# One run of scores and one run of outputs per chunk in place of four mixed runs, in decayed linear attention with a softplus feed-forward

## The chip, the cores and the metric

One core of a Trainium2 chip runs the whole kernel. The metric is the device time of one execution in microseconds (us); the time of a kernel is the median of its runs. Differences under about 0.2% are at the edge of what repeated runs can tell.

## The reference

Attention with a decay per head, computed block by block (block of 64 positions) with a state that is carried along the sequence, and then a feed-forward layer with softplus over all tokens. `q`, `k`, `v` are (4, 8, 768, 64): batch, heads, positions, head size.

```python
for b in range(nb):                       # nb = 768 / 64 blocks
    intra = einsum('bhic,bhjc->bhij', qb, kb) * Dmask        # scores in the block
    intra = einsum('bhij,bhjd->bhid', intra, vb)
    inter = einsum('bhid,bhde->bhie', qb * lam_pow, kv_state)
    out[block] = intra + inter
    kv_state = lam_block * kv_state + einsum('bhsd,bhse->bhde', kb * rev_pow, vb)
x = out as (4 * 768 tokens, 512)
h = x @ w_in                              # (512, 2048)
g = maximum(h, 0) + log1p(exp(-abs(h)))   # softplus
return g @ w_out                          # (2048, 512)
```

## The kernel before

**Tiling.** The sequence is cut into 6 chunks of 128 positions (two blocks of 64). In a chunk the 8 heads form 4 pairs. A *unit* `g` is one pair in one chunk, `g = 4 * chunk + pair`, 24 in all. Its `q`, `k`, `k` transposed and `v` for all 4 batches lie in one tile `att{g}`.

**The feed-forward part** goes in slots `s = 16 * chunk + f`, one for each chunk and each of 16 slices of the hidden layer. `mlp1(s)` (L344) makes `h` with 12 matmuls of 128x512; ScalarE takes the softplus into `l` (L334) and casts its high half into `g` (L338), VectorE subtracts to get the low half (L342); four slots later `mlp2(s)` (L358) adds 12 matmuls of 128x512 into the four banks `o` of the chunk, one for each batch. After the sixteenth slot of a chunk the four banks are copied out (L376) and stored. The split into a high and a low half is for precision: each product is made of three.

**The attention part** of a unit has these steps. `k_decay` (L262, ScalarE) scales the transposed keys. `mm_scores` (L276, L278, TensorE) makes the scores `x` and the sums for the state `y`, 64 small matmuls of 64x64. `mask_scores` (L297, VectorE) writes the masked scores over `k`. `update_states` (L302, VectorE) makes the state at the second block, and the state for the next chunk's unit of the same pair. `q_decay` (L267, VectorE) scales `q`. `mm_out` (L289, L293, TensorE) makes the outputs `z`, again 64 small matmuls. `x_high` and `x_low` (L318 on ScalarE, L325 on VectorE) split `z` into the input of the next chunk's `mlp1`.

**Buffers.** PSUM's 8 banks are divided for the whole program: four `o`, two `h`, and two as one tile `t` ("work"). In SBUF a pool of 22 tiles of 8 KB per partition holds units, weights, the inputs `x_{chunk}` and the output buffer `ob`; a pool of 7 tiles of 4 KB holds the `g`; one tile holds `l`; five hold states.

**What sets the order.** The program is written out in order; each engine does its own instructions in that order and waits by semaphores. The first stage (chunk 0, the conversion of the weights, the units of chunk 1) follows a table written out by hand (L476 to L505). From slot 17 on a loop (L517) works: every fourth slot it has an *event* for one unit `g`, in which TensorE does the outputs of unit `g - 1` and the scores of unit `g` one behind the other, and then an `mlp2` and two `mlp1`. So a chunk has four such mixed runs of small matmuls among its large ones, and attention is one chunk ahead of the feed-forward part. Transfers are issued from SP's queue in program order.

## Time and profile before

| | us |
|---|---|
| median of 3 runs | 595.84 |
| lowest and highest | 595.80 and 596.04 |
| the profiled execution | 595.62 |
| its span, first to last instruction | 593.8 |

The profiled execution has 1.8 us outside its span. The profile shows one execution. Engines are PE (TensorE's matmuls), PEld (its weight loads), DVE (VectorE), ACT (ScalarE), POOL (GpSimd) and SP (the queue that issues transfers). In its rows "L353" is line 353 of the kernel, `h<-x,w` names what is written and read, and "x12" counts instructions. In a timeline a row's start and its duration in us stand first; matmuls overlap in the array, so the distance between starts tells the pace, and not the duration of one (some 390 ns for a large one).

### The profile page before, as it was taken

How to read it: one execution, taken by the hardware profiler on the slowest of the kernel's cores; microseconds unless marked ns; L12 is line 12 of the kernel's file. 1: busy time of each engine (PE TensorE's matmuls, PEld its weight loads, DVE VectorE, ACT ScalarE, POOL GpSimd, SP SyncE). 2: the span in 40 equal slices, each digit the busy share in tenths (PEclk: the TensorE clock that was granted, in tenths of full speed). 3: DMA queues.
4: the chain of work that ended last, by engine and by line, in shares of the span. 5: the costliest groups of instructions: out<-in, count | busy, mean ns of one | idle time of the engine just before them, and what ended most of it. 6: DMA issues, size and time to landing. Idle time of an engine off the chain costs nothing.

```text
span 593.8 us, 11190 instructions
## 1 busy us (share of the span) xinstructions
PE 586.9 (99%) x5009; PEld 484.3 (82%) x5009; DVE 224.3 (38%) x338; ACT 210.0 (35%) x341; POOL 1.5 (0%) x9
## 2 busy tenths in 40 slices
PE   8999999999999999999999999999999999999997
PEld 6778888888888888888888888888888888888885
DVE  8999999623313134132232331312312211211011
ACT  5899867232233232322323213323232222222211
POOL 1000000000000000000000000000000000000000
PEclk9999999999999999999999999999999999999999
DMA  8999230214002106001022300220500000100001
GB/s 288 416 416 418 106 131 2 72 73 142 3 0 72 73 0 214 0 2 52 21 72 90 124 3 0 73 72 0 214 0 2 1 0 1 72 0 2 0 1 71
DMA packets 15759, 48.95 MB, mean 82 GB/s; under 512 B 1888, under 2 KB 1888, under 8 KB 15712
## 3 DMA queue, kind: packets, MB, share of 16 engines
q1 hardware_dynamic: 15344, 47.46, 21.4%
q10 hardware_dynamic: 368, 0.79, 0.4%
q8 instruction: 39, 0.64, 0.4%
q14 instruction: 8, 0.07, 0.0%
HBM read 41.95 MB, written 6.29 MB: 81 GB/s over the span
## 4 chain that ended last, share of the span: by engine, by line
PE 94%; DMA 3%; DVE 1%; SPq 1%; issue 0%; ACT 0%
PE o L370 45%; PE h L353 42%; PE x L276 2%; PE z L289 2%; PE z L293 2%; DMA att<-in_att 1%; DMA raw<-in_wts 1%; PE y L278 1%; DVE c L219 1%; DVE w L232 0%; DVE c L215 0%; DVE c L225 0%; PE y L440 0%; SPq L122 0%; PE w L276 0%
## 5 line engine op out<-in xcount | busy, mean ns | idle before, releaser
L370 PE MATMUL o<-w,g 128*128 128x512 f32 x1152 | 278.6, 392 | 0.0
L353 PE MATMUL h<-x,w 128*128 128x512 f32 x1152 | 274.5, 390 | 0.3 <-ACT x L417 0.3
L353 PEld LDWEIGHTS h<-x,w 128*128 128x128 f32 x1152 | 215.8, 188 | 46.4 <-DVE w L232 0.7
L370 PEld LDWEIGHTS o<-w,g 128*128 128x128 f32 x1152 | 214.8, 188 | 45.3
L342 DVE TENSOR_TENSOR g<-l,g 128x512 fp32r<-128x512 f32 x96 | 66.4, 692 | 305.3 <-ACT g L338 305.3
L334 ACT ACTIVATE l<-h 128x512 f32<-128x512 f32 x96 | 57.5, 598 | 310.9 <-PE h L353 308.6
L338 ACT CAST g<-l 128x512 fp32r<-128x512 f32 x96 | 59.6, 621 | 2.8
L302 DVE SCALAR_TENSOR_TENSOR st<-st,lam_c,y 64x256 f32<-64x256 f32 x68 | 29.9, 480 | 2.4 <-PE y L278 1.3
L297 DVE TENSOR_TENSOR att<-x,mask 128x512 f32<-128x512 f32 x19 | 13.1, 692 | 43.4 <-PE y L278 23.8
L318 ACT CAST x<-z 128x512 fp32r<-128x512 f32 x20 | 11.7, 585 | 41.4 <-PE z L293 41.4
L289 PEld LDWEIGHTS z<-att,st 64*64 64x64 f32 x640 | 17.0, 134 | 7.0 <-issue 6.3
L276 PE MATMUL x<-att 64*64 64x64 f32 x608 | 21.7, 219 | 0.0
L278 PE MATMUL y<-att 64*64 64x64 f32 x544 | 21.3, 219 | 0.0
L289 PE MATMUL z<-att,st 64*64 64x64 f32 x640 | 20.9, 224 | 0.0
L225 DVE CUSTOM_DVE_ANT_0 c<-raw,c 128x2048 uint16<-128x2048 uint16 (+1 forms) x19 | 20.0, 1054 | 0.3
L276 PEld LDWEIGHTS x<-att 64*64 64x64 f32 x608 | 20.1, 135 | 0.0
L232 DVE TENSOR_TENSOR w<-c,w 128x1024 fp32r<-128x1024 f32 (+1 forms) x19 | 20.0, 1055 | 0.1
L219 DVE SCALAR_TENSOR_TENSOR c<-raw,c 128x1024 uint32<-128x1024 uint32 (+1 forms) x19 | 20.0, 1053 | 0.0
L207 ACT ACTIVATE c<-raw 128x1024 f32<-128x1024 f32 (+1 forms) x19 | 18.9, 1006 | 3.1 <-DMA raw<-in_wts 3.1
L293 PE MATMUL z<-att 64*64 64x64 f32 x640 | 19.9, 218 | 0.0
L278 PEld LDWEIGHTS y<-att 64*64 64x64 f32 x544 | 19.6, 135 | 0.0
L211 ACT ACTIVATE raw<-raw 128x1024 uint32<-128x1024 uint32 (+1 forms) x19 | 19.1, 1013 | 1.2 <-DMA raw<-in_wts 1.2
(48 smaller groups left out, 172.6 us busy)
## 6 DMA issues: line engine op xcount, KB each, us to landing
att<-in_att SPq DMA_DIRECT2D x43, 512.0 KB, 4.9
raw<-in_wts SPq DMA_DIRECT2D x32, 512.0 KB, 9.2
out_dram<-ob SPq DMA_DIRECT2D x22, 256.0 KB, 2.3
att<-in_att SPq DMA_DIRECT2D x9, 256.0 KB, 7.5
out_dram<-ob ACTq DMA_DIRECT2D x2, 256.0 KB, 2.0
att<-in_att ACTq DMA_DIRECT2D x1, 256.0 KB, 4.7
lam_b<-in_lam SPq DMA_DIRECT2D x1, 4.0 KB, 2.8
```

Of the source, the lines that this page charges most:

```text
L219: nc.vector.scalar_tensor_tensor(out=c, in0=raw_at(ks, 1), scalar=0x80000000, in1=c, op0=ALU.bitwise_and, op1=ALU.bitwise_or)
L225: nc.vector.tensor_add(out=c, in0=c, in1=raw_at(ks, 0))
L276: nc.tensor.matmul(x[r, cols], lhsT=k[r, b, t], rhs=q[r, b, t], start=True, stop=True)
L278: nc.tensor.matmul(y[half(1 - s), cols], lhsT=kd[r, b, t], rhs=v[r, b, t], start=True, stop=True)
L289: nc.tensor.matmul(w[half(t), s, cols], lhsT=st[r, b, t], rhs=qd[r, b, t], start=True, stop=False)
L293: nc.tensor.matmul(w[half(t), s, cols], lhsT=v[r, b, t], rhs=a[r, b, t], start=False, stop=True)
L302: nc.vector.scalar_tensor_tensor(out=to[:, :, t], in0=of[:, :, t], scalar=lam_c[r, h : h + 1], in1=u[:, :, t], op0=ALU.mult, op1=ALU.add,)
L334: nc.scalar.activation(l_tiles[s], h_tiles.pop(s), AF.Softplus)
L338: nc.scalar.copy(out=g_tiles[s][:, 0, :], in_=l_tiles[s])
L342: nc.vector.tensor_sub(out=g[:, 1, :], in0=l_tiles.pop(s), in1=g[:, 0, :])
L353: nc.tensor.matmul(h_tiles[s], lhsT=w[:, i, cs], rhs=x[:, j, :], start=p == 0 and n == 0, stop=p == NP - 1 and n == 2,)
L370: nc.tensor.matmul(o_tiles[c][b], lhsT=g[:, i, b * 128 : (b + 1) * 128], rhs=w[:, j], start=f == 0 and n == 0, stop=f == NF - 1 and n == 2,)
```

## The change

In the loop the four events of a chunk become two.

- **Scores.** In the fourth slot of a chunk (`f == 3`), behind the last `mlp2` of the chunk before, TensorE does the scores and state sums of all four units of the next chunk (`chunk_scores`), 256 small matmuls. They fill all 8 banks: the two `h` for the first unit, the four `o` for the second and third, the work tile for the fourth. VectorE masks and updates unit by unit. The `mlp2` of the next slot is put off by one slot, since it needs the `o` banks.
- **States.** The two states of a unit are now written into the place of its transposed keys (`update_kept`): ScalarE copies the carried state there, VectorE makes the second one beside it.
- **Decays.** `k_decay` of the four units goes into slots 1 to 3 of the chunk, `q_decay` into slots 4 to 7.
- **Outputs.** In slot 8 TensorE does the outputs of all four units (`chunk_outs`), 256 small matmuls, two units to a pair of banks: the two `h`, and the work tile. Casts and subtractions then take a whole bank of two units at a time.
- **Loads.** Two units are loaded behind the outputs, the other two in slot 1 of the next chunk.
- **Output buffer.** It is made of four tiles of the 4 KB pool, in place of one of the 8 KB pool.
- **The table.** Its steps for unit 8 (`kd1 8`, `sc1 8`, `m1 8`, `up 8`, `qd 8`) are gone; the loop does them.

```diff
-    def mm_out(g, w):
+    def mm_out(g, w, first=0):
...
+    def update_kept(g, y):
+
+        u = y.rearrange("q (b t e) -> q b t e", b=B, t=2)
+        old, st = states[g], kt_of(g)
+        states[g] = st
+        nc.scalar.copy(out=st[lo], in_=old[lo])
+        decayed(g, st[hi], old[lo], lo, u[hi])
+        if not last_chunk(g):
+            states[g + NP] = th([128, B, 2, D], F32, f"st_{g + NP}")
+            decayed(g, states[g + NP][lo], st[hi], hi, u[lo])
+
+    def chunk_scores(c):
+
+        homes = [(bank, bank), (obank, obank), (obank, obank), None]
+        for g, home in zip(range(c * NP, c * NP + NP), homes):
+            if home:
+                xy[g] = [new(f"{name}{g}") for new, name in zip(home, "xy")]
+            else:
+                w = work(f"w{g}")
+                xy[g] = w[:, 0], w[:, 1]
+            mm_scores(g, *xy[g])
+
+    def chunk_outs(c):
+
+        homes = {0: [bank(f"z{c}_{s}") for s in range(2)]}
+        w = work(f"z{c}")
+        homes[1] = [w[:, s] for s in range(2)]
+        for p in range(NP):
+            mm_out(c * NP + p, homes[p // 2], p % 2 * 256)
...
+            for s in range(2):
+                nc.scalar.copy(out=x[:, 0, s], in_=of[s])
+            for s in range(2):
+                nc.vector.tensor_sub(out=x[:, 1, s], in0=of[s], in1=x[:, 0, s])
...
-            ob = t8([128, B, 512], F32, f"ob{c}")
+            ob = [t4([128, 2, 512], F32, f"ob{c}_{i}")[:, j] for i in range(2) for j in range(2)]
...
     for s in range(17, last + LAG):
-        if events.get(s + 1, NG) < NG:
-            run("kd1", events[s + 1])
+        c, f = divmod(s, NF)
+        first = (c + 1) * NP
+        if f == 1 and c < NCH - 1:
+            load_upto(first + NP)
+        if 1 <= f <= 3 and c < NCH - 1:
+            for g in ((first,), (first + 1,), (first + 2, first + 3))[f - 1]:
+                run("kd1", g)
...
-        if s in events:
-            g = events[s]
-            run("out1", g - 1)
-            if g < NG:
-                run("sc1", g)
...
+        if f != LAG or c == NCH:
+            mlp2_upto(s - LAG)
+        if f == LAG - 1 and c < NCH - 1:
+            chunk_scores(c + 1)
+            for g in range(first, first + NP):
+                mask_scores(g, xy[g][0])
+                update_kept(g, xy[g][1])
+        if f in range(LAG, 2 * LAG) and c < NCH - 1:
+            run("qd", first + f - LAG)
+        if f == 2 * LAG and c < NCH - 1:
+            chunk_outs(c + 1)
+            mlp2_upto(s - LAG + 1)
+            load_upto(first + NP + 2)
         if s < last:
             mlp1(s)
```

How this stands on the engines is shown at two places. First TensorE at the end of a run that has scores. Before, in the loop, the scores of unit 18 (`x18`, `y18`) end the mixed run, and one `mlp2` (into `o3`) and two `mlp1` (into `h56`, `h57`) follow:

```order
L276 MATMUL x18_3321<-att18_3175 64x64
L278 MATMUL y18_3322<-att18_3175 64x64
L370 MATMUL o3_0_3070<-w7_722,g53_3211 128x512 x3
L370 MATMUL o3_1_3071<-w7_722,g53_3211 128x512 x3
L370 MATMUL o3_2_3072<-w7_722,g53_3211 128x512 x3
L370 MATMUL o3_3_3073<-w7_722,g53_3211 128x512 x3
L353 MATMUL h56_3379<-x_3_0_2334,w6_573 128x512 x6
L353 MATMUL h56_3379<-x_3_1_2737,w6_573 128x512 x6
L353 MATMUL h57_3397<-x_3_0_2334,w7_722 128x512 x6
L353 MATMUL h57_3397<-x_3_1_2737,w7_722 128x512 x6
```

Now the scores of units 16 to 19 end with unit 19 in the work tile (`w19`); two `mlp1` (lines of the changed kernel: L391) take the two `h` banks, and then comes the `mlp2` that opens the chunk's `o3`:

```order
L276 MATMUL w19_3136<-att19_2934 64x64
L278 MATMUL w19_3136<-att19_2934 64x64
L391 MATMUL h51_3197<-x_3_0_2662,w1_264 128x512 x6
L391 MATMUL h51_3197<-x_3_1_2667,w1_264 128x512 x6
L391 MATMUL h52_3216<-x_3_0_2662,w2_360 128x512 x6
L391 MATMUL h52_3216<-x_3_1_2667,w2_360 128x512 x6
L408 MATMUL o3_0_3234<-w2_360,g48_2941 128x512 x3
L408 MATMUL o3_1_3235<-w2_360,g48_2941 128x512 x3
L408 MATMUL o3_2_3236<-w2_360,g48_2941 128x512 x3
L408 MATMUL o3_3_3237<-w2_360,g48_2941 128x512 x3
```

Behind the small matmuls stands now an `mlp1`, whose bank the scores of unit 16 hold, and the `mlp2` comes third.

Second VectorE around the same units. Before, each unit's mask and state steps stand alone between the low halves of two slots, with the subtraction of the unit before and the scaling of `q`:

```order
L342 TENSOR_TENSOR g55_3273<-l55_3271,g55_3273 128x512
L297 TENSOR_TENSOR att18_3175<-x18_3321,mask_104 128x512
L302 SCALAR_TENSOR_TENSOR st_18_2540<-st_18_2540,lam_c_108,y18_3322 64x4x64 x2
L302 SCALAR_TENSOR_TENSOR st_22_3359<-st_18_2540,lam_c_108,y18_3322 64x4x64 x2
L325 TENSOR_TENSOR x_4_0_3153<-z17_3288,x_4_0_3153 128x2x4x64
L267 TENSOR_TENSOR att18_3175<-att18_3175,lp_105 128x512
L342 TENSOR_TENSOR g56_3394<-l56_3392,g56_3394 128x512
```

Now, behind the output copies of the chunk before (L414; the rows are from the second copy on), two of the four units in their new order:

```order
L414 COPY ob2_1_3013<-o2_3_2413 128x512
L297 TENSOR_TENSOR att16_2684<-x16_3034,mask_104 128x512
L302 SCALAR_TENSOR_TENSOR att16_2684<-st_16_2349,lam_c_108,y16_3035 64x4x64 x2
L302 SCALAR_TENSOR_TENSOR st_20_3173<-att16_2684,lam_c_108,y16_3035 64x4x64 x2
L297 TENSOR_TENSOR att17_2687<-x17_3068,mask_104 128x512
L302 SCALAR_TENSOR_TENSOR att17_2687<-st_17_2356,lam_c_108,y17_3069 64x4x64 x2
L302 SCALAR_TENSOR_TENSOR st_21_3180<-att17_2687,lam_c_108,y17_3069 64x4x64 x2
```

Twelve rows of this kind, four units, stand on VectorE one behind the other, and the low half of the slot's `g` (`g51`) comes only behind them.

## The prediction

> **What bounds the kernel now.** I read the page first: engine shares, the slices, the chain that ended last.

> ```profile
> span 593.8 us, 11190 instructions
> ...
> PE 586.9 (99%) x5009; PEld 484.3 (82%) x5009; DVE 224.3 (38%) x338; ACT 210.0 (35%) x341; POOL 1.5 (0%) x9
> ...
> PEclk9999999999999999999999999999999999999999
> ...
> PE 94%; DMA 3%; DVE 1%; SPq 1%; issue 0%; ACT 0%
> ```

> TensorE is the bound: 94% of the chain is its own work, the granted clock is full in every slice, and the chain's other engines belong to the start. So only two things can move the time after the first chunks: what TensorE spends, and a wait that the new order gives it. Next the table of waits:

> ```profile
> ACT l L334 <- PE h L353: 308.6, 86, 6.1
> ...
> PEld z L289 <- issue: 6.3, 18, 0.4
> ```

> The other engines wait for TensorE. TensorE's own repeated gap is the second row: 18 times its weight loads stood still for 6.3 / 18 = 0.35 us before L289, the first line of a run of small matmuls, and no semaphore released it. That is a price of entering such a run. The whole price is read from TensorE's timeline (start, duration, line). The last run of the program holds outputs alone:

> ```profile
> 485.27 2.88 PE L370 MATMUL o<-w,g 128*128 128x512 f32 x12
> ...
> 490.71 2.88 PE L370 MATMUL o<-w,g 128*128 128x512 f32 x12
> 493.52 0.34 PE L289 MATMUL z<-att,st 64*64 64x64 f32 x8
> ...
> 493.80 0.30 PE L289 MATMUL z<-att,st 64*64 64x64 f32 x8
> ...
> 494.27 0.30 PE L289 MATMUL z<-att,st 64*64 64x64 f32 x8
> ...
> 494.61 3.02 PE L370 MATMUL o<-w,g 128*128 128x512 f32 x12
> 497.47 2.88 PE L353 MATMUL h<-x,w 128*128 128x512 f32 x12
> ```

> From 485.27 to 490.71 lie 24 large matmuls without a break: 5.44 us, 0.227 each. From 490.71 to 497.47 lie 24 large ones and one output run: 6.76 us, so the run costs 6.76 - 5.44 = 1.32 us. Inside it, 32 small matmuls pass between 493.80 and 494.27: 0.47 us, 0.0147 each, so its 64 are worth 0.94. The remaining **0.38 us is paid per run, not per matmul**: the first small one starts late, and the twelve large ones after it take 497.47 - 494.61 = 2.86 in place of 2.72. A mixed run of the loop (outputs of one unit, scores of the next) shows the same:

> ```profile
> 250.24 2.88 PE L370 MATMUL o<-w,g 128*128 128x512 f32 x12
> 253.06 0.34 PE L289 MATMUL z<-att,st 64*64 64x64 f32 x8
> ...
> 255.10 3.02 PE L370 MATMUL o<-w,g 128*128 128x512 f32 x12
> 257.96 1.30 PE L353 MATMUL h<-x,w 128*128 128x512 f32 x5
> ```

> 7.72 - 5.44 = 2.28 us, 0.96 more than the run of outputs alone, for 64 more matmuls: 0.015 each and no second price between the two kinds.

> **The change part by part.**

> *Fewer runs.* Before, the loop makes 16 small runs (15 mixed, one of outputs). After, it makes two for each of four chunks, 8. The written list keeps one run at its end (outputs of unit 7); the scores of unit 8 that stood behind them there go into the loop's first long run. The number of small matmuls is the same, 128 a unit. Gain: 8 x 0.38 = **3.0 us**, all on TensorE's path.

> *Waits inside a run.* Each unit's scores wait for its own buffers and transfers, even if these came long ago. The cheapest and the dearest mixed run of the loop bound what that does to a running sequence:

> ```profile
> 226.23 2.88 PE L370 MATMUL o<-w,g 128*128 128x512 f32 x12
> ...
> 233.92 1.30 PE L353 MATMUL h<-x,w 128*128 128x512 f32 x5
> 442.54 2.88 PE L370 MATMUL o<-w,g 128*128 128x512 f32 x12
> ...
> 450.33 1.98 PE L353 MATMUL h<-x,w 128*128 128x512 f32 x8
> ```

> 7.69 and 7.79, so 2.25 and 2.35: 0.10 apart. In the new score runs three of four units start behind other scores, 12 in all: 0 to 12 x 0.10 = 1.2 us. The mixed runs paid some of this already, and 2.28 is nearer to the low end, so I take **+0.2**, and keep 0 to 1.2.

> *The eight banks.* A score run fills all of PSUM, so large matmuls can resume only as VectorE empties it. Durations by group, and VectorE's timeline behind one run:

> ```profile
> L342 DVE TENSOR_TENSOR g<-l,g 128x512 fp32r<-128x512 f32 x96 | 66.4, 692 | 305.3 <-ACT g L338 305.3
> L334 ACT ACTIVATE l<-h 128x512 f32<-128x512 f32 x96 | 57.5, 598 | 310.9 <-PE h L353 308.6 <-DVE g L342 2.0
> L318 ACT CAST x<-z 128x512 fp32r<-128x512 f32 x20 | 11.7, 585 | 41.4 <-PE z L293 41.4
> L325 DVE TENSOR_TENSOR x<-z,x 128x512 fp32r<-128x512 f32 x20 | 13.8, 689 | 2.9 <-ACT x L318 2.5
> L376 DVE COPY ob<-o 128x512 f32<-128x512 f32 x12 | 8.3, 689 | 8.8 <-PE o L370 8.2
> ```

> ```profile
> 279.24 0.69 DVE L297 TENSOR_TENSOR att<-x,mask 128x512 f32<-128x512 f32 x1 [2.78 <-PE y L278]
> 279.97 1.79 DVE L302 SCALAR_TENSOR_TENSOR st<-st,lam_c,y 64x256 f32<-64x256 f32 x4
> 281.79 0.69 DVE L325 TENSOR_TENSOR x<-z,x 128x512 fp32r<-128x512 f32 x1
> ```

> One unit's mask and four state steps take 281.79 - 279.24 = 2.55 us. Count from the start of a score run. Its end is 4 x 0.95 = 3.8. VectorE has two output copies first (0.69 each, the second from about 0.2), then the first mask from about 1.2, and is through with units one to four at 3.75, 6.3, 8.85 and 11.4. TensorE asks: the first `h` bank at 3.8 (its scores are masked at 1.9), the second one `mlp1` later, 3.8 + 0.2 + 2.72 = 6.7 (free at 3.75); the four `o` banks at 9.4 and each 0.68 on, the last at 11.4 (free at 8.85). The smallest cover is 1.9 us. The low half of that slot's `g`, queued on VectorE behind all four units, is done at 12.1; until then it holds the only `l` buffer, so the next softplus ends at 12.7, and TensorE needs that bank at 9.4 + 4 x 2.72 = 20.3. An output run fills the two `h` banks by its middle, 1.9; two casts (0.585) and two subtractions (0.69) empty them by about 4.1; the next `mlp1` wants one after 3.8 + 0.2 + 2.72 = 6.7. If VectorE were later than these covers, each us beyond would be TensorE's, up to four times over. **Cost taken: 0.**

> *Additions off the path.* Sixteen copies of half a state on ScalarE; the nearest row is the cast, 0.585, so at most 16 x 0.585 = 9.4 us on an engine that is busy 35% and, in the loop, waits for TensorE before each softplus. They stand ahead of the softplus of the slot, but finish with the scores, before that slot's `mlp1` does. The output buffers become four pieces from the smaller pool; the next `g` tiles wait for their transfers, which land in 2.3 us against a need after more than 7.

> ```profile
> att<-in_att SPq DMA_DIRECT2D x43, 512.0 KB, 4.9
> ...
> out_dram<-ob SPq DMA_DIRECT2D x22, 256.0 KB, 2.3
> ...
> lam_b<-in_lam SPq DMA_DIRECT2D x1, 4.0 KB, 2.8
> ```

> Two units are now loaded together one slot into a chunk, four transfers of 512 KB on SP's queue; ScalarE decays them two slots later, 4 x 2.72 = 10.9 us after their buffers are free. At 4.9 for one and twice that for a crowd they are in time. In this stage the load stands ahead of the output stores, so it does not wait for them. Cost taken: 0.

> *Sum.* -3.0 + 0.2 = -2.8. The profiled execution took 595.62, 0.22 below the median of 595.84; from the median that is **593.0**.

> **The rivals.**

> *A. Code arrives too slowly (slower).* The page's queue table:

> ```profile
> q8 instruction: 39, 0.64, 0.4%
> ```

> 39 packets for 2 x 5009 TensorE instructions are 257 each: a mixed run of 256 uses up about one, in 1.9 us. The new runs of 512 use two on end. If only one is fetched ahead, the second must come within 1.9 us; the smallest transfer above took 2.8, so each of 8 runs would stand 0.9: 7.2 - 2.8 = +4.4, **600.2**. It decides from 2.8 / 8 = 0.35 us a run. Against it: mixed runs cross such borders at 0.015 a matmul without a visible stop. For it: no run in this trace crosses two in a row. [...] Chance 0.09.

> *B. The waits cost more.* If every later unit of a score run pays the dearest 0.10 us, 1.2 in place of 0.2: **594.0**; if the queue ahead of TensorE does not refill within a run, twice that, 595.2. Chance 0.13.

> *C. The price per run is not saved.* If the entry price were the drain of work already queued, or were paid again between units because the run's tiles and banks change, eight prices come back: 3.0, and **595.8**, no change. Against it: outputs to scores inside a mixed run costs nothing extra. Chance 0.06.

> *D. The clock drops in a long run.* Small matmuls use a quarter of the array each; the longest stretch so far is 1.9 us, at full clock. If 3.8 us counted as idle and the clock halved for as long again, 8 x 1.9 = 15 us: **608**. Chance 0.02. [...]

> **How the numbers follow.** My forecast, 593.0, has 0.70; its own range is 592.2 (0.42 a run, no added waits: 595.84 - 3.4 is 592.4, and 0.2 of noise) to 594.0. B reaches to 595.0 for most of its chance. So 592.2 to 595.0 holds about 0.81; A, C and D lie outside. Differences under 0.2% (1.2 us) can hardly be told from none here; that line lies at 594.65. Faster: the forecast and most of B, 0.81. Same: C and the tail of B, 0.08. Slower: A, D and unforeseen waits, 0.11.

> **What would show it.** Right: 8 rows of idle before L289 and L276 in the loop in place of 16 before L289, each run of 256 small matmuls 4.1 to 4.2 us by the same subtraction (256 x 0.0147 + 0.38), and no wait of TensorE for VectorE or ScalarE in the loop. A shows as a gap inside a run with no releaser; B as runs of scores dearer than runs of outputs; C as a run of 4.9 us or more; D in the clock row. A row of TensorE waiting for VectorE behind a score run would make the eight-bank step wrong.

## The result, and the profile after

The changed kernel takes **604.47 us** (median of four; the undisturbed three 604.07 to 604.79) against 595.94 for the kernel before in the same session: ratio 1.014, 95% interval 1.012 to 1.016. The forecast was 593.0, range 592.2 to 595.0. It was wrong in sign, and the outcome is rival A's, some 4 us beyond its price.

The first profiled execution of the changed kernel was disturbed (1812 us; TensorE's large matmuls start some 0.69 us apart in place of 0.227, throughout) and the ratio leaves it out; all rows of this kernel below are from a second profile.

> The changed kernel once more, for a profile of an execution that is not disturbed. If the 8.4 us by which it was slower (604.4 against 595.9) are a stop inside the long runs of small matmuls (code that comes too late, or waits that pile up), the eight runs take about 1 us more each than 256 x 0.0147 + 0.38 = 4.15 us, and the large matmuls keep their 0.227 us. If TensorE's clock is lowered, the large matmuls behind the runs get slower or the clock row shows it. If a buffer comes too late, TensorE waits for VectorE or ScalarE behind a score run.

Measured: 605.22 (603.90 to 606.62) against 595.69, ratio 1.0153 (1.0136 to 1.0170). The profiled execution took 606.62, its span 604.8, which is 11.0 more than the span before. The page first:

```profile
span 604.8 us, 11277 instructions
...
PE 589.6 (97%) x5009; PEld 487.7 (81%) x5009; DVE 223.6 (37%) x338; ACT 218.9 (36%) x357; POOL 1.5 (0%) x9
...
PEclk9999999999999999999999999999999999999999
...
PE 93%; DMA 3%; issue 2%; DVE 1%; SPq 1%; ACT 0%
```

The number of matmuls is the same, VectorE's work is the same, ScalarE has its 16 copies more. What is new is "issue 2%" in the chain that ended last: 2% of the span in which TensorE was next to go, and nothing that the profile shows held it. The table of waits says where (engine, line, releaser; total us, times, longest):

```profile
PEld w L278 <- issue: 4.4, 2, 2.2
...
PE w L278 <- issue: 4.1, 2, 2.1
...
PEld z L289 <- issue: 3.2, 7, 1.1
PEld z L293 <- issue: 3.0, 2, 1.7
```

Before, the longest wait of this kind was 0.4 us, and it stood ahead of a run. These are up to 2.2 us long, and L278 and L293 are lines inside a run. No row there has TensorE waiting in the loop for VectorE or ScalarE, and among its starts in the loop no other step is long. TensorE's timeline at the first long run of the loop shows one of them from near by:

```profile
129.87 0.22 PE L278 MATMUL w<-att 64*64 64x64 f32 x1
129.90 0.22 PE L276 MATMUL w<-att 64*64 64x64 f32 x1
132.21 0.27 PE L278 MATMUL w<-att 64*64 64x64 f32 x1 [2.09 <-issue]
132.21 0.27 PE L276 MATMUL w<-att 64*64 64x64 f32 x1
```

Two neighbours of the same unit, of the same tile, with the same buffers, start 2.31 us apart. A bank, a mask or a transfer of data is hard to see here: what the second one needs, its neighbours needed too. What the trace does have in this run is one packet of instructions (queue 8). It starts at 128.99, takes 1.82 us, and TensorE goes on 1.40 us after its end:

```profile
q8 instruction: 1, 0.02, 1.8%
```

The other five stops have such a packet too. Next a table of windows (start:end; its length and how much of it TensorE was busy, with the instructions; granted clock; busy share of the DMA engines, GB/s). It has the six long stops, two long runs with hardly a stop, and the stretches after the first and the fifth stop:

```profile
129.90:132.21 2.31, 0.22 (x15) 1.00 0.03 8
165.35:166.54 1.19, 0.22 (x13) 1.00 0.22 65
230.42:232.04 1.62, 0.22 (x16) 1.00 0.05 13
263.52:264.93 1.41, 0.21 (x14) 1.00 0.29 81
328.83:331.06 2.23, 0.22 (x15) 1.00 0.04 10
364.09:365.83 1.74, 0.22 (x16) 1.00 0.36 118
426.29:430.49 4.20, 4.20 (x194) 1.00 0.67 254
457.63:462.09 4.46, 4.46 (x259) 1.00 0.03 7
...
132.93:136.80 3.87, 3.87 (x12) 0.56 0.02 4
...
332.49:334.36 1.87, 1.87 (x6) 0.50 0.00 0
```

Six stops add up to 2.31 + 1.19 + 1.62 + 1.41 + 2.23 + 1.74 = 10.5 us, and the DMA engines are nearly idle in the two longest of them (busy shares of 0.03 and 0.04). The last two rows are a second effect: after the two longest stops, and after no other, the granted clock is half (0.50 in the last row), and the large matmuls start 427 ns apart in place of 227. That costs some 1.7 us each time (in the first, nine steps take 3.75 us in place of 2.04). The page's clock row hides it, since one of its slices is 15 us long. It does not come in every execution: their mean granted clocks are 0.994, 0.997, 0.997 and 1.000, which is two such stretches, one, one and none, at 606.62, 605.08, 605.37 and 603.90 us. The rows from 426.29 and 457.63 are the two long runs that go through, in 4.20 and 4.46 us from the last large matmul ahead to the first behind. The first of them, the scores of the last chunk, leaves out state sums and has 192 matmuls, so 384 instructions; the second has 512 like the six that stop.

The budget closes: -2.8 (the forecast's sum) + 10.5 + 0.15 (a small stop in the run at 457.63) + 2 x 1.7 = +11.2, against 11.0 measured.

### The profile page after: what moved, and what is told of

Its sections match the earlier page's. It is cut to its first block, busy times and chain, and to the rows that moved or that the text cites. A ratio compares the mean times of both kernels' runs of the same rounds, so it can differ in the third digit from the quotient of the medians.

```text
span 1810.5 us, 11277 instructions
## 1 busy us (share of the span) xinstructions
PE 1805.4 (100%) x5009; PEld 1046.1 (58%) x5009; DVE 226.0 (12%) x338; ACT 218.9 (12%) x357; POOL 1.5 (0%) x9
## 4 chain that ended last, share of the span: by engine, by line
PE 100%; DVE 0%; issue 0%
PE h L391 46%; PE o L408 45%; PE x L276 2%; PE z L289 2%; PE z L293 2%; PE warm_ps L146 1%; PE x L434 1%; PE z L449 1%; PE w L276 1%; PE y L278 1%; PE y L478 0%; PE w L278 0%; DVE ob L414 0%; DVE warm L141 0%
## 5 line engine op out<-in xcount | busy, mean ns | idle before, releaser
L391 PE MATMUL h<-x,w 128*128 128x512 f32 x1152 | 844.0, 969 | 0.0
L408 PE MATMUL o<-w,g 128*128 128x512 f32 x1152 | 835.7, 959 | 0.0
L391 PEld LDWEIGHTS h<-x,w 128*128 128x128 f32 x1152 | 450.9, 392 | 365.9 <-issue 363.4
L408 PEld LDWEIGHTS o<-w,g 128*128 128x128 f32 x1152 | 446.3, 388 | 358.8 <-issue 356.3
L380 DVE TENSOR_TENSOR g<-l,g 128x512 fp32r<-128x512 f32 x96 | 66.4, 691 | 1248.6 <-ACT g L376 1248.5
L376 ACT CAST g<-l 128x512 fp32r<-128x512 f32 x96 | 59.4, 619 | 18.6 <-PE o L408 15.9
L293 PE MATMUL z<-att 64*64 64x64 f32 x640 | 50.5, 427 | 0.0
L276 PEld LDWEIGHTS x<-att 64*64 64x64 f32 x480 | 44.4, 356 | 4.3 <-issue 4.3
L276 PE MATMUL x<-att 64*64 64x64 f32 x480 | 45.2, 419 | 0.0
L278 PE MATMUL y<-att 64*64 64x64 f32 x432 | 45.2, 420 | 0.0
L278 PEld LDWEIGHTS y<-att 64*64 64x64 f32 x432 | 44.4, 363 | 0.0
L293 PEld LDWEIGHTS z<-att 64*64 64x64 f32 x640 | 44.3, 352 | 0.0
L289 PE MATMUL z<-att 64*64 64x64 f32 x512 | 39.1, 415 | 0.0
L289 PEld LDWEIGHTS z<-att 64*64 64x64 f32 x512 | 34.0, 338 | 5.1 <-issue 5.1
L297 DVE TENSOR_TENSOR att<-x,mask 128x512 f32<-128x512 f32 x15 | 10.4, 692 | 86.8 <-PE x L276 54.3
## 6 DMA issues: line engine op xcount, KB each, us to landing
att<-in_att SPq DMA_DIRECT2D x43, 512.0 KB, 4.7
raw<-in_wts SPq DMA_DIRECT2D x32, 512.0 KB, 7.5
out_dram<-ob SPq DMA_DIRECT2D x22, 256.0 KB, 2.0
att<-in_att SPq DMA_DIRECT2D x9, 256.0 KB, 7.5
out_dram<-ob ACTq DMA_DIRECT2D x2, 256.0 KB, 2.0
att<-in_att ACTq DMA_DIRECT2D x1, 256.0 KB, 4.8
```

The source lines that it names most:

```text
L276: nc.tensor.matmul(x[r, cols], lhsT=k[r, b, t], rhs=q[r, b, t], start=True, stop=True)
L278: nc.tensor.matmul(y[half(1 - s), cols], lhsT=kd[r, b, t], rhs=v[r, b, t], start=True, stop=True)
L289: nc.tensor.matmul(w[s][half(t), cols], lhsT=st[r, b, t], rhs=qd[r, b, t], start=True, stop=False)
L293: nc.tensor.matmul(w[s][half(t), cols], lhsT=v[r, b, t], rhs=a[r, b, t], start=False, stop=True)
L376: nc.scalar.copy(out=g_tiles[s][:, 0, :], in_=l_tiles[s])
L380: nc.vector.tensor_sub(out=g[:, 1, :], in0=l_tiles.pop(s), in1=g[:, 0, :])
```

## The experiments

Two theories to begin with. **Theory 1**: the stops are waits for code. TensorE's instructions would come in blocks of 256 (39 packets for its 10018 instructions; with a weight load for each matmul, 128 matmuls), with only one block ahead; a run that uses up blocks faster than they come would stop at the end of one, a *border*. **Theory 2**: it is the run itself or what the change did around it, its banks and data, or more small matmuls on end than some queue bears.

**Large matmuls in the middle of each long run.** Eight useless matmuls of 128x512 stand between the second and the third unit of every long run. `fill` writes them to the work tile before its own small matmuls do; their results are not used.

```diff
         for g, home in zip(range(c * NP, c * NP + NP), homes):
+            if g % NP == 2:
+                fill(w[:, 0], c)
...
         for p in range(NP):
+            if p == 2:
+                fill(w[:, 0], c)
             mm_out(c * NP + p, homes[p // 2], p % 2 * 256)
```

> The changed kernel with 8 large matmuls of no use put into the middle of each of its 8 long runs (between the second and the third unit). Their work is 8 x 0.227 us and one more price of 0.38 for leaving and entering, 2.2 us a run, 17.5 us in all. Theory 1 (code comes too late: a block of 256 TensorE instructions must be there before the one ahead of it is used up, and the long run uses one in 1.9 us): the added time covers the stop, the stops of 1.2 to 2.3 us go, and so does the lowered clock behind them; 605.2 + 17.5 - 10.7 - 2 = about 610. Theory 2 (the stop is a wait of the scores for buffers, or a price per run length): the added work comes on top, 605.2 + 17.5 = 622.7.

Measured: 610.69, ratio 1.0256 (1.0240 to 1.0271), span 608.8. The waits of TensorE for "issue", the longest single one last in each row:

```profile
PEld x L276 <- issue: 2.8, 8, 0.4
PEld z L289 <- issue: 2.1, 6, 0.4
...
PEld w L278 <- issue: 0.2, 1, 0.2
```

The long stops are gone (the one row on L278 has 0.2 us left of 4.4), and no stretch at half clock is left (the mean granted clock is 1.000). 64 matmuls of 0.227 and eight more entries into a run were added, 14.5 + 3 = 17.5, and the profiled span rose by only 608.8 - 604.8 = 4.0. So 13.5 us went, near the 10.65 of stops and 3.4 of half clock that the changed kernel's profile had. That is Theory 1's number. But a wait for a bank or for data would be covered by the added time as well, and a price on the length of a run would go with the cut: this run does not part the theories, the shifted ones and the last one below do.

**Each long run in two halves.** The rest of the change stays (the states in the unit's tile, the decays in advance, the loads; the banks are dealt out anew), but there are four runs of 256 instructions per chunk, with large matmuls between.

```diff
-            chunk_scores(c + 1)
+            chunk_scores(c + 1, (0, 1))
...
+        if f == LAG and c < NCH - 1:
+            chunk_scores(c + 1, (2, 3))
...
-            chunk_outs(c + 1)
+            chunk_outs(c + 1, (0,))
             mlp2_upto(s - LAG + 1)
+            chunk_outs(c + 1, (1,))
```

> The changed kernel with each long run cut into two of two units (256 TensorE instructions), with feed-forward matmuls between the halves, all else as in the change: states in the unit's tile, banks, output buffers, decays ahead. Theory 1 (code): four runs a chunk as before, no stop, 595.7, within 0.7. Theory 2 (the new places of states, decays and buffers make TensorE wait): the loss stays, 600 or more.

Measured: 596.58, ratio 1.0013 (1.0004 to 1.0022). No stop inside a run, so nothing else of the change costs several us. It is 0.9 above Theory 1's number, a little outside the 0.7 allowed, and the table of waits has a row for that, with VectorE's timeline beside it:

```profile
PEld o L412 <- issue: 1.4, 3, 0.5
```

```profile
137.97 0.87 DVE L302 SCALAR_TENSOR_TENSOR st<-att,lam_c,y 64x256 f32<-64x256 f32 x2
138.88 0.69 DVE L267 TENSOR_TENSOR att<-att,lp 128x512 f32<-128x512 f32 x1
```

In the three full chunks the `mlp2` behind the second half stands twice, 0.3 us in all each time. In this kernel unit 3's sums lie in an `o` bank, VectorE's last state step of it ends at 138.84, and TensorE's matmul into that bank starts at 138.99. So here VectorE is late by 0.3 us, as far as the two timelines tell; no run takes this wait away by itself. In the change unit 3 lies in the work tile, and there is no such wait. The profile's word "issue" does not name the cause in this row.

**Three runs per chunk.** If a run of 384 instructions has a border near its middle, it uses part of one block and part of the next, and Theory 1 lets it pass. The scores of units 0 to 2 make one run; the outputs of units 0 and 1 and the scores of unit 3 the second; the outputs of units 2 and 3 the third. Banks, loads and one `q_decay` move with them.

```diff
+            chunk_scores(c + 1, (0, 1, 2))
...
+        if f == 11 and c < NCH - 1:
+            chunk_outs(c + 1, (0,))
+            chunk_scores(c + 1, (3,))
...
+        if f == 14 and c < NCH - 1:
+            chunk_outs(c + 1, (1,))
```

> Three runs a chunk: scores of three units (384 instructions), outputs of two and scores of the fourth (384), outputs of two (256). By the count of instructions ahead of them, the border of a block falls near the middle of both runs of 384 (192 instructions in), so no block lies wholly inside one. Theory 1 (code): no stop, and 12 runs in place of 16 save 4 x 0.38 = 1.5 us against the kernel before: 594.2. If only the length of a run matters, and not where the border falls, runs of 384 stop about half as long as runs of 512: 600.

Measured: **593.88** (593.81 to 594.14), ratio 0.9969 (0.9956 to 0.9981), faster than both kernels. Its runs as windows, from the last large matmul ahead to the first behind:

```profile
126.55:129.85 3.30, 3.30 (x195) 1.00 0.85 315
173.27:176.55 3.28, 3.28 (x195) 1.00 0.02 5
192.78:195.12 2.34, 2.34 (x130) 1.00 0.03 7
```

No run stops. 192 matmuls take 3.28 and 128 take 2.34, which is 0.0147 each, the forecast's price.

**The same kernel, shifted against the borders.** 48 matmuls (96 instructions) more at the start of the program move every later run by 96 of 256 against the borders of the blocks.

```diff
-    keep_warm(13)
+    keep_warm(12)
+    for _ in range(49):
+        nc.tensor.matmul(warm_ps[:, 0:32], lhsT=warm[:, :128], rhs=warm[:, :32], start=True, stop=True)
```

> The same kernel with 48 more TensorE matmuls (96 instructions) in the warm-up at the program's start, and nothing else changed. Theory 1 (code): the border moves 96 instructions forward in every run behind it, two borders fall into each run of 384, a whole block lies inside, and 8 runs stop 1.2 to 2.3 us each: 604 to 612. Every other theory: the same as without them, within 1 us.

Measured: 611.09, ratio 1.0266 (1.0249 to 1.0283). This number must not be taken for the shift's: the run of outputs that stands at 106.19 before the shift is at 113.41 here, so 7.2 us were lost at the start. There the added matmuls take 7.5 us, and from 9.45, while they run, to 19.69 the granted clock is half. The rest is stops, the first two and the last of six (in all 7.2 + 9.0 of the 16.7 us by which the span is longer):

```profile
136.76:138.63 1.87, 0.22 (x14) 1.00 0.15 50
185.37:186.95 1.58, 0.22 (x15) 1.00 0.63 140
...
383.12:384.11 0.99, 0.21 (x12) 1.00 0.11 25
sum 9.00, PE 1.31; mean PE 0.22
```

All six runs of 384 instructions, which had passed without a stop, now stand 1.0 to 1.9 us, 9.0 in all. (The two like runs of the last chunk leave out state sums, have 288 and 352 instructions, and pass.) Counted in the trace, the stops come behind matmuls 1364, 1746, 2255, 2638, 3147 and 3529. In the changed kernel, whose runs are other ones at other places of the program, they come behind 1363, 1745, 2253, 2635, 3144 and 3526. So it is the number of the instruction that decides, and no place of the program. (The spacing, 382 to 383 and 508 to 509, is a little under a multiple of 128 matmuls; the trace has 55 to 65 other instructions on TensorE's queue, which would count too.) From this the rule for these runs can be said more sharply: **a run goes over its first border freely and stops at the second**. The runs of 384 had one border in them and now have two; the runs of 512 always have two.

One run of 512 nearly escapes it, the one at 457.63 in the changed kernel: it stood 0.15 us at its second border, behind matmul 4290. Counted back by 127 matmuls, its first border lies 22 matmuls into the run, where it lies 84 to 101 into the six that stopped. The packet for the second border started at 458.11, 2.05 us ahead of the stop, in place of 0.7 to 1.2. So here and in the six the stop is as long as the packet's way to TensorE (2.05 + 0.15 = 2.2 us from its start to the next matmul here, 2.3 to 3.2 in the six), less the work that is left ahead of the border when the packet starts.

**A shift that leaves the start alone.** Because of that delay, 48 useless matmuls of 64 columns were put into slot 18 instead, in the stage that TensorE bounds, with a control of six matmuls of 512 columns (12 instructions) at the same place; the diff shows the 48.

```diff
+        if s == NF + 2:
+            pad = work("pad")
+            for _ in range(48):
+                nc.tensor.matmul(
+                    pad[:, 0, 0:64], lhsT=w_of(0, 0)[:, 0, 0:128], rhs=x_of(c, 0)[:, 0, 0:64],
+                    start=True, stop=True,
+                )
```

> The kernel of three runs per chunk (593.88), with 48 added matmuls of 64 columns (96 instructions) behind the mlp2 of slot 18, in the stage that TensorE bounds, so that the start isn't touched. They do useless work worth 48 x 0.027 to 0.030 = 1.3 to 1.4 us, and 0.4 for the entry at most. Theory 1 (blocks of 256 instructions, one ahead): every later run sits 96 instructions on against the block borders, as in the run shifted at the start, so the runs of 384 instructions in chunks 2 to 4 again stand 1.0 to 1.9 us each, six stops, 9 us in all: 593.9 + 1.8 + 9 = 604.7, between 602 and 606. Theory 2 (where the borders fall doesn't matter, and the shifted run was slow for its late start alone): 595.3 to 595.7 and no stop.

> The control for the run with 48 added matmuls: 6 added matmuls of 512 columns at the same place, 6 x 0.227 = 1.36 us of the same useless work, but only 12 instructions, so the borders move by 12 of 256. Both theories: 593.9 + 1.4 = 595.2 to 595.6, no stop over 0.3 us in a run. If it too takes over 600, it is the added work at this place, and not the position of the borders, that costs.

Measured: 611.58, ratio 1.0257 (1.0240 to 1.0274), for 48 matmuls, and 595.17, ratio 0.9989 (0.9980 to 0.9998), for six. The windows of the first: the added work, the stretch behind it, and the six stops, with the stretch behind the third of them:

```profile
121.27:126.40 5.13, 5.13 (x48) 1.00 0.00 0
126.83:130.21 3.38, 3.38 (x10) 0.51 0.00 0
136.36:138.46 2.10, 0.22 (x16) 1.00 0.17 56
...
235.82:238.01 2.19, 0.21 (x13) 1.00 0.17 58
239.57:242.56 2.99, 2.99 (x9) 0.50 0.00 0
...
385.03:386.58 1.55, 0.21 (x12) 1.00 0.42 116
```

The control is where both theories had it. The shifted one has the six stops at the same numbers (1364, 1746, 2255, 2638, 3147, 3529), 10.2 us in all. It missed its expectation by 7 us for two reasons that the theories don't differ on: the 48 matmuls took 5.1 us in place of 1.4 (an estimate that 0.227 x 64/512 us for each would give), as they start 112 ns apart (so did the 49 of 32 columns in the run before, while the clock was full); and the clock was halved twice, behind these 48 and behind the stop of 2.19 us, at 1.6 to 1.7 us each. Stops, added work and half clock make 10.2 + 5.3 + 3.3 = 18.8 of the 19.2 us by which its span is longer than that of the three runs.

**The price of a block by itself.** At the end of the kernel before, three runs of useless small matmuls, with 24 large ones ahead of each: 640 calls of 64 columns, 320 of 128, 160 of 256 (each such call makes two matmuls), so 1280, 640 and 320 matmuls. There is one execution, the profiled one.

```diff
+    for n, calls in ((64, 640), (128, 320), (256, 160)):
+        w = work(f"probe{n}")
...
+                    nc.tensor.matmul(
+                        w[half(t), r, 0:n], lhsT=k[half(r), j % 4, t], rhs=units[g][half(r), 0, 0, 0:n],
+                        start=True, stop=True,
+                    )
```

> The kernel before, with three long runs of small matmuls of no use behind its end, each behind 24 large matmuls: 1280 matmuls that move 64 columns (10 blocks of 256 instructions), 640 that move 128 (5 blocks), 320 that move 256 (2.5 blocks). Nothing in them waits. Theory 1 (code): the runs of 64 columns stop once in every 256 instructions, and go at the pace of the blocks, some 3.3 us each as the stops in the changed kernel tell (1.9 us of work and 1.2 to 2.3 of stop, less the lead), so about 33 us in place of 18.8; the runs of 128 columns, whose work is about 3.8 us a block, stop little or not; those of 256 not at all. If the stops come from the scores' waits or from transfers of the loop, no run stops.

The three runs as windows of that line (TensorE's matmuls and weight loads), and two bursts of the first run in the timeline:

```profile
595.54:632.21 36.67, 20.74 (x1280) 19.59 (x1280) 1.00 0.01 4
638.18:655.61 17.43, 17.43 (x639) 17.43 (x640) 1.00 0.01 4
661.64:678.76 17.12, 17.12 (x320) 12.14 (x320) 1.00 0.01 2
```

```profile
603.22 2.09 PE L562 MATMUL probe<-att 64*64 64x64 f32 x128 [1.64 <-issue]
607.22 2.09 PE L562 MATMUL probe<-att 64*64 64x64 f32 x128 [1.91 <-issue]
```

```profile
q8 instruction: 9, 0.15, 1.5%
```

0.15 MB / 9 is 16 KB a packet; if it holds the 256 instructions of a burst, 64 bytes each. So a block came within 3.49 us where nothing stopped, and took 3.7 to 4.0 where TensorE stood and waited for it.

The trace also has the time of each packet, and this ties every stop to its block. In all 27 long stops (six each in the changed kernel and in the two shifted ones, nine here) a packet starts 0.2 to 1.2 us ahead of the stop and takes 0.9 to 1.8 us, and TensorE goes on 1.2 to 1.6 us after its end. From the packet's start to the next matmul that is 2.2 to 3.2 us, also in the run that stood only 0.15.

## Why the prediction was wrong

**Fewer runs: the price was right, the step failed in what a run is.** Three runs in place of four, and the forecast's 0.38 a run, make the kernel of three runs 16 to 12 runs, 4 x 0.38 = 1.5 us faster; it is 2.0 faster (the other 0.5 was not taken apart). The run of 256 matmuls that goes through takes 4.46; by the prediction's own subtraction (the first step behind a run is 0.11 too long) and without the small stop that is 4.2, where 4.1 to 4.2 stood. (The run of 192 comes out at 4.09 the same way, where 192 x 0.0147 + 0.38 is 3.2: without the state sums a matmul took 0.020. No experiment is about that.) What failed is the step that gives all eight runs 256 x 0.0147 + 0.38 and takes the saving of 3.0 as the whole effect on TensorE. The 0.0147 was read from runs of 256 instructions and carried to runs of 512. Six of the eight long runs contain a stop of 1.2 to 2.3 us.

**Rival A was the mechanism, at a chance of 0.09 and a price of 0.9 us a run.** The point against it, that mixed runs cross borders at full pace, was no evidence: every run in these traces crossed its first border freely, since that block came while the large matmuls ran (ahead of the first long run its packet ended at 117.78, 8.8 us before the run began). 128 large matmuls last 29 us (128 x 0.227), over seven times the 3.7 to 4.0 us that a block took in the probe. Only a second border in the same run tests it, and the prediction itself noted that no run of the trace has one. A ground "against" which holds under the rival too should have weighed nothing. The price came from the smallest data transfer, 2.8 us to land, less 1.9 us that a block lasts. The 2.8 was near, by luck, as it is a transfer of another kind: from the packet's start to the next matmul 2.3 to 3.2 us pass in the six stops. The 1.9 was wrong: the packet does not start when the block ahead begins, but only 0.7 to 1.2 us ahead of the stop. So 1.2 to 2.3 is missing in place of 0.9: seven stops, 10.65 us, in place of 7.2 for eight.

**Rival D in part.** It was priced as a clock that falls in every long run. It fell behind two of six stops: those of 2.31 and 2.23 us, some 1.7 us each. Small matmuls of 64x64 by themselves did not bring it down: the two long runs that go through keep a granted clock of 1.00, and behind the probe's run of 128 columns, 17 us long, the large matmuls start 0.227 us apart. (The probe's trace has no record of the clock, and its 1.00 in the windows says nothing.)

**Waits inside a run: right, as far as read.** In the kernel of halves a run of two units' scores takes 2.37 us where a run of two units' outputs takes 2.34, so 0.03 for the one unit that starts behind another: 12 x 0.03 = 0.4, near the 0.2 taken and far from the 1.2 feared. So rival B is not what happened.

**The eight banks: right**, and this step had the most working in it. VectorE's first mask starts 1.2 us behind the run's start (127.84 to 126.61), and it is through with the four units 11.4 us behind it, as worked out. No row shows TensorE waiting for a bank there. (With the stop in the run TensorE came later, so this cover was not fully tried; the kernel of three runs, without stops, has no such wait either.)

**Additions off the path: right.** ScalarE has 8.9 us more work, and it waits for TensorE as before.

**Rival C** did not happen: long runs that go through pay their price once, and a step between two kinds inside a run costs nothing that shows (3.28 us for the run of outputs and scores in the kernel of three, 3.30 to 3.33 for scores alone).

## What to carry to other kernels

Before small matmuls are gathered into longer runs, count instructions, not only time: how many 256-instruction blocks does the run hold, and how long does one last in it? At 1.9 us a block a run went over one border freely and stopped at the second; at 3.5 it did not stop; what lies between was not tried. Runs of 256 instructions were safe here, runs of 384 by luck of their position, and of seven runs of 512 one got away with 0.15 us. Large matmuls between the halves mended it. And when a rival is dismissed because "the trace shows it working", ask whether the trace ever came to the case that the rival speaks of.

## What the runs showed of the hardware that was not expected

- **Position decides.** 96 instructions more, far ahead of the runs that they touch, turn a kernel of 593.9 into one with six stops and 9 to 10 us more. Twelve instructions more cost nothing but their time (595.17, 1.3 us for 1.36 of work). So the kernel of three runs is faster, but fragile: an edit elsewhere on TensorE can cost four to five times its gain of 2.0 us.
- **A short stand can halve the clock, and its place decides.** The clock record has every halving in the loop at 3.41 us, and the changes of one trace lie whole multiples of that apart (133.18 to 331.15 is 58 of them). So the trace can be cut into windows of 3.41 us from any change. In the kernel with 48 added matmuls, TensorE's busy time in some of them:

```profile
123.46:126.87 3.41, 3.41 (x31) 1.00 0.00 0
126.87:130.28 3.41, 3.41 (x10) 0.50 0.00 0
137.11:140.52 3.41, 2.06 (x24) 1.00 0.05 14
236.10:239.51 3.41, 1.50 (x26) 1.00 0.07 18
239.51:242.92 3.41, 3.41 (x9) 0.50 0.00 0
```

  Behind the window with 1.50 us of work the next one is at half clock; so it was in the changed kernel behind windows with 1.32 and 1.40. The stop of 2.10 us at 136.36 is cut by the window's edge at 137.11, leaves 2.06 us of work, and halves nothing; the least work in the loop that halved nothing is 1.76 us, in the kernel shifted at the start. But the first two rows show that busy time is not all: a window full of matmuls of 64 columns at 112 ns each is followed by half clock too.
- **"issue" has at least three meanings** in these traces: the entry into a run (0.35 us), a wait for code (1.0 to 2.3 us), and, in the kernel of halves, most likely a wait for a bank whose releaser the profile missed (0.3 us). Length and place in the run tell them apart.
